# Three edits to a kernel of attention and two expert layers: weight loads behind the last maxima, the last tile's y in two parts, and one second layer ahead of transposes

## The chip, the cores and the metric

The kernel runs on one core of a Trainium2 chip. Its time is device microseconds (us) of one execution, median of several. The core has a matrix engine (TensorE, PE in the profile, its weight loads PEld), VectorE (DVE), ScalarE (ACT), GpSimd (POOL) and SyncE (SP), which here issues most of the transfers. Each engine works through a program of its own in order, and waits for the others by semaphores.

## The reference

Three stages follow each other, all in float32:

```python
def _attn_ref(q, k, v, f):            # (4, 8, 576, 64), f: (4, 8, 576)
    scores = q @ k.transpose(0, 1, 3, 2) / sqrt(D)
    cum = np.cumsum(np.log(np.clip(f, 0.0001, 1.0)), axis=-1)
    scores = np.where(causal, -1e9, scores + cum[..., :, None] - cum[..., None, :])
    scores = scores - np.max(scores, axis=-1, keepdims=True)
    attn = np.exp(scores)
    return attn / (np.sum(attn, axis=-1, keepdims=True) + 1e-09) @ v

def _moe_ref(x, w1, w2, w3, w_out):   # x: (2304, 512), w3: (1024, 1024)
    return ((x @ w1) * (x @ w2) @ w3) @ w_out

def _moe2_ref(x, w_gate, w_output_gate, w1, w2):   # 8 experts, 512 -> 1024 -> 512
    e_idx = np.argmax(x @ w_gate, axis=1)          # one expert for each row
    ...
    out[mask] = gate_w * eom * (np.maximum(x[mask] @ w1[e], 0.0) @ w2[e])
```

## The kernel before

**Precision.** Most operands are split in a high part (a reduced float32 form, fp32r) and a low part (the rest), and a product takes three matmuls: high by high, high by low, low by high (`three`, lines 549 to 551).

**Attention** goes over 16 pairs of heads, n = 0 to 15. What is done for a pair is cut into steps ("X0": scores of a row block, "m0": its maxima, "GA": the scores again, transposed, into PSUM group gA, "HA": the maxima and the decay added to it by matmuls from MR and CK, "eA": exponential, "a0": causal mask, "s1": block sums on POOL, "p0": product with v, "su": sums of the weights). Steps of one pair lie up to 90 us apart; each has a start time in `START`, pair n is 9.8 us behind pair n−1, and every engine's program is this list sorted by time. The last block of 64 queries is handled for both heads at once ("XL", tile xl). Its maxima end the row maxima of the pair: they are turned by a matmul and copied to the tile mt ("tc", ACT, line 253), and SP moves them into MR ("mv", line 183). gA's matmuls with MR and CK wait for that.

**The weights w3 and w_out** are multiplied with each other while attention runs, so that the gated layer needs one product y instead of two. They come in pieces of 512 KB (o0, 00, o1, ...; class `Combined`). A piece goes through seven steps, K0 to K6 (`narrow`, lines 449 to 467): SP loads it, ACT, DVE (lines 458, 460, 462) and ACT convert it from 64-bit to 32-bit floats, POOL takes the low part. `upto(step, n)` issues a step for the first n pieces. The raw buffers are three, so a load waits until DVE has read the piece three before it. In attention's program the steps of the pieces stand in the same list; those at its end stand in `AFTER`, in us after the start of the last pair: "K0_15" is the load of the 15th piece (w14), "K0_16" that of wo5, "K0_17" that of w05, "K4_13" and "K4_14" are the conversions of wo4 and w04. P0 to P3 are the first products of the two matrices.

**The gated layer** (`gated`) takes 512 rows at a time, the last tile (t=4) 256. For each f of eight it makes a and b, their product ga, and its parts gh and gl (`post`, on ACT and DVE). `project` then makes y for each chunk of 128 rows from all eight f (24 matmuls of 512 columns), copies it to a row tile xr with ACT, turns it by four transposes (`turn`), and, in `rest`, makes the logits; `route` finds the expert of each row and its place, and POOL scatters the rows into xs, sorted by expert. PSUM tiles of these stages come from five buffers in turn (`mmt`).

**The experts.** The most frequent expert m comes first: its first 256 rows ("A", `layer1`, then `layer2` with both chunks), then 128 more ("B", `features` with four transposes, `layer1_few`, `turn_few`, `layer2`), then the other seven. The order of PE's and DVE's work is as written here, with generators that are advanced by `take` and `run`; ACT, POOL and SP are ordered by a planner. `weights` asks for weight chunks of 512 KB, through three raw buffers; each `load` splits one on POOL and DVE. `fetch` brings rows from xs; those of B (xgB) are fetched on POOL's queue behind the scatter of the last tile's rows.

Of the kernel before, what the change touches and what calls it, by code (L numbers as in the profile page):

```python
# [11 lines left out]
F32 = mybir.dt.float32  # L12
# [15 lines left out]
E = 8  # L28
P = 128
# [32 lines left out]
FILL = {(0, "X0"): 5, (0, "XL"): 10, (1, "X0"): 4, (1, "XL"): 4, (2, "X2"): 5, (2, "X0"): 5}  # L62

AFTER = {
    "K4_13": 4.4, "K0_15": 4.41, "K0_16": 4.42, "K4_14": 4.43, "K0_17": 4.44, "inputs": 11.36, "scores": 13.38,
    "K1_15": 18.5, "K1_16": 18.51, "K4_15": 18.52, "K0_18": 18.53, "K4_16": 18.54, "P0": 28.29, "P1": 28.3, "P2": 28.31,
    "P3": 28.32,
}
# [449 lines left out]
def moe(nc, tc, ident, xT, rz, xs, xpool, raws, region, wc, w1, w2, gates, e1, e2, out):  # L518
# [3 lines left out]
    with (  # L522
# [12 lines left out]
        def mmt(name):  # L535
            return st["mm"].tile([P, 512], F32, name=name, tag="mm")

        def tmp(name):
            return st["work"].tile([P, 512], F32, name=name, tag="tmp", bufs=TMP if "moa" in st else 3)
# [5 lines left out]
        def three(ps, terms, start=True, stop=True):  # L545

            last = len(terms) - 1
            for i, ((ah, al), (bh, bl)) in enumerate(terms):
                PE.matmul(ps, ah, bh, start=start and i == 0, stop=False)  # L549
                PE.matmul(ps, ah, bl, start=False, stop=False)  # L550
                PE.matmul(ps, al, bh, start=False, stop=stop and i == last)  # L551

        TT = [512] * 4 + [N - 2048]
# [52 lines left out]
            return st["xr"][:, c % 2]  # L606

        def project(t, nc_):
            rows, lg = [], psr.tile([P, 4, 2 * E], F32, name=f"lg{t}", tag="r")
            if t == len(TT) - 1:  # L610
                x2t = [p2.tile([P, 2, P * nc_], F32, name=f"x2t{k}", tag="ga") for k in (0, 2)]
            else:
                x2t = [xT[:, k:k + 2, 512 * t:512 * t + P * nc_] for k in (0, 2)]

            def rows_of(c):
                cs = slice(P * c, P * c + P)
                ps = mmt(f"y{t}{c}")
                three(ps, [((gh[:, f, cs], gl[:, f, cs]), (wch[:, f], wcl[:, f])) for f in range(8)])
                rows.append(row_tile(t, c))
                A.activation(out=rows[c][:, :DM], in_=ps, func=ACTF.Copy)  # L620

            def turn(c):
                pt = psx.tile([P, 512], F32, name=f"xt{t}{c}", tag="x")
                for k in range(4):
                    PE.transpose(pt[:, P * k:P * k + P], rows[c][:, P * k:P * k + P], ident)
                for i, y in enumerate(x2t):
                    A.activation(out=y[:, :, P * c:P * c + P], in_=pt[:, 256 * i:256 * i + 256].rearrange("p (k c) -> p k c", k=2), func=ACTF.Copy)

            for c in range(nc_):
                rows_of(c)  # L630
                if c > 0:
                    turn(c - 1)

            def rest():
                turn(nc_ - 1)
                yield

                pt = psx.tile([P, 512], F32, name=f"lt{t}", tag="x")
                for k in range(4):
                    PE.matmul(pt[32 * k:32 * k + 32, :P * nc_], wg[:, k], x2t[k // 2][:, k % 2], start=True, stop=True)  # L640
                part = tmp(f"lp{t}")
                A.activation(out=part[:, :P * nc_], in_=pt[:, :P * nc_], func=ACTF.Copy)
                yield
                for c in range(nc_):
                    PE.matmul(lg[:, c], part[:, P * c:P * c + P], four, start=True, stop=True)
                yield
                yield from route(t, nc_, rows, lg)

            return rest()
# [78 lines left out]
        w1h, w1l, w2h, w2l, gh, gl = (unit(x, 8) for x in ("w1h", "w1l", "w2h", "w2l", "gh", "gl"))  # L728
# [6 lines left out]
        for hf, j in wc.steps:  # L735
# [12 lines left out]
            if j == 7:  # L748
                if hf == 0:
                    wch, wcl = (x.bitcast(F32R) for x in wc.raw)  # L750
# [7 lines left out]
        psr = psum.enter_context(tc.tile_pool(name="psr", bufs=1, space=PSUM, reuse_waits="tile"))  # L758
# [316 lines left out]
        def rows_of_expert(e, first=0):  # L1075
            return lambda r, n: by_expert[bass.ds(e, 1), first + r:first + r + n].rearrange("o n d -> (o n) d")

        def run(*steps):

            for x in steps:  # L1080
                for _ in x:
                    pass

        def take(x, n=1):
            for _ in range(n):
                next(x, None)

        m = nc.values_load(mi[0:1, 0:1], engines=[*SPE, POOL_E], min_val=0, max_val=E - 1)
        with tc.manual_schedule(engines={PE_E, DVE_E}):
            wm, gA = weights("m", m), fetch("A", rows_of_expert(m), 256)  # L1090
            fA = features("A", gA, 256)
            xA, hA = next(fA), hidden("A")
            rest = project(len(TT) - 1, TT[-1] // P)
            load(4)
            take(fA, 2)
            take(rest)
            take(fA, 2)
            take(rest)
            l1 = layer1("A", wm, xA, 256, hA)
            take(l1)  # L1100
            take(rest, 2)
            cn = count("")
            next(cn)
            take(l1, 2)
            run(rest)
            gB = fetch("B", rows_of_expert(m, 256), P, "xgB", 1, G)
            take(l1)
            load(1)
            take(l1)
            pl = plan(*next(cn))  # L1110
            load(1)
            take(pl)
            take(l1)
            load(1)
            take(l1)
            load(1)
            slots = [None] + [nc.values_load(tab[0:1, i:i + 1], engines=SPE, min_val=0, max_val=E - 1) for i in range(1, 3)]
            take(l1)
            ws = weights("1", slots[1])
            g = fetch("1", rows_of_expert(slots[1]), WIN[1])  # L1120
            run(l1)
            y = layer2("A", wm, gA, hA, 256)
            fB = features("B", gB, P)
            xB, hB = next(fB), hidden("B")
            take(y, 2)
            run(fB)
            run(y)
            load(2)
            hr = layer1_few("B", wm, xB)
            fx = features("1", g, WIN[1])  # L1130
            x = next(fx)
            take(fx, 2)
            turn_few("B", hr, hB)
            take(fx, 2)
            load(2)
            run(layer2("B", wm, gB, hB, P))
            load(1)
            h = hidden("1")
            l1 = layer1("1", ws, x, WIN[1], h)
            for _ in range(3):  # L1140
                take(l1, 1)
                load(1)
            slots += [nc.values_load(tab[0:1, i:i + 1], engines=SPE, min_val=0, max_val=E - 1) for i in range(3, E)]
            for i in range(1, E):
                nm, w = str(i), WIN[i]
                if i == E - 1:
                    pe0 = nc.values_load(tab[0:1, E:E + 1], engines=SPE, min_val=0, max_val=E - 1)
                    px0 = nc.values_load(tab[0:1, E + MAXP:E + MAXP + 1], engines=SPE, min_val=0, max_val=E * N - R)
                    nm2, e2_, w2_, rows2 = "p", pe0, R, lambda r, n: xs[bass.ds(px0, n)]
                else:  # L1150
                    nm2, e2_, w2_, rows2 = str(i + 1), slots[i + 1], WIN[i + 1], rows_of_expert(slots[i + 1])
                g2 = fetch(nm2, rows2, w2_)
                ws2 = (weights if i < E - 1 else plain)(nm2, e2_)
                if i > 1:
                    h = hidden(nm)
                    l1 = layer1(nm, ws, x, w, h)
                    take(l1)
                for k in range(4):
                    take(l1, 2 if i > 1 else 1)
                    load(1 if i < E - 1 else 0)  # L1160
                run(l1)
                fx = features(nm2, g2, w2_) if i < E - 1 else iter(())
                x = next(fx, None)
                take(fx, 2)
                y = (layer2_turned if w % P and w <= TURNED else layer2)(nm, ws, g, h, w)
                if i < E - 1:
                    take(y)
                    take(fx, 2)
                    for k in range(4):
                        load(1)  # L1170
                        take(y)
                        take(pl)
                else:
                    x = turned_piece("p", g2)
                    take(y)
                    p = piece("p", ws2, g2, x)
                    for _ in range(2):
                        take(p)
                        take(y)
                run(y)  # L1180
                ws, g = ws2, g2
            run(p)
# [61 lines left out]
```

## Time and profile before

| | |
|---|---|
| Time, median of 3 runs | 846.82 us (845.28 to 849.52) |
| The profiled execution | 848.34 us, its span 846.7 us |
| PE busy | 799.8 us, 94% |
| DVE, POOL, ACT busy | 451.4 us (53%), 376.2 us (44%), 281.3 us (33%) |
| Mean granted clock of PE | 0.986 of full speed |

Attention lasts until about 205 us, the products of the two weight matrices until about 262, the gated layer with y until about 580, the experts until the end. Times in the rows count from the start of the span. "L579" is line 579 of the kernel before.

### The profile page before, as it was taken

The numbers are of one execution on the slowest core, as the hardware profiler recorded it, in microseconds if no ns is written. First come the engines' busy times: TensorE is split into PE (matmuls) and PEld (weight loads), VectorE is DVE, ScalarE is ACT, GpSimd is POOL, SyncE is SP. The second block draws the span as 40 slices with busy tenths as digits, with TensorE's granted clock in tenths as the row PEclk, the third lists the DMA queues.
The fourth block names the chain that finished last, engine by engine and source line by source line (L and its number), as shares of the span: only waits on it lengthen the run. The fifth ranks groups of instructions, "written<-read, shape, count | busy, mean of one in ns | idle before, by whom it ended". The sixth has DMA issues, their size and how long they took to land.

```text
span 846.7 us, 13835 instructions
## 1 busy us (share of the span) xinstructions
PE 799.8 (94%) x5173; PEld 648.9 (77%) x5173; DVE 451.4 (53%) x950; ACT 281.3 (33%) x536; POOL 376.2 (44%) x383
## 2 busy tenths in 40 slices
PE   8999979969999899999999999999799999999995
PEld 4666656647886587787788788888588899999983
DVE  7788878862897841340423222245356846446530
ACT  2666656624354422212221221222122222322321
POOL 5688888875465550230113011032345443444521
PEclk9999999988999999999999999999999999999999
DMA  3455666521544220110100010043556654556460
GB/s 114 153 169 188 215 209 217 155 94 44 180 166 137 90 64 12 51 28 11 38 25 19 7 51 0 1 133 117 187 175 194 213 199 144 188 187 210 151 258 29
DMA packets 40340, 102.12 MB, mean 121 GB/s; under 512 B 8610, under 2 KB 9314, under 8 KB 40016
## 3 DMA queue, kind: packets, MB, share of 16 engines
q1 hardware_dynamic: 37088, 91.46, 33.9%
q0 software_dynamic: 3184, 9.77, 3.0%
q8 instruction: 41, 0.67, 0.3%
q14 instruction: 27, 0.22, 0.1%
HBM read 84.47 MB, written 16.51 MB: 119 GB/s over the span
## 4 chain that ended last, share of the span: by engine, by line
PE 60%; DVE 16%; DMA 11%; issue 7%; ACT 3%; SPq 2%; POOL 1%; POOLq 0%; DVEq 0%; ACTq 0%
DVE junk L243 5%; PE y L551 4%; PE y L550 4%; PE y L549 4%; PE h L551 3%; PE h L549 3%; PE h L550 3%; PE a L549 3%; PE b L549 3%; DMA xs<-xr,pos 3%; PE a L551 3%; PE a L550 3%; PE b L550 3%; PE b L551 3%; DMA out<-ot,id 3%
## 5 line engine op out<-in xcount | busy, mean ns | idle before, releaser
L579 DVE TENSOR_TENSOR ga<-b,ga 128x512 f32<-128x512 f32 (+1 forms) x40 | 25.4, 635 | 150.8 <-PE b L551 147.7
L694 POOL DMA_INDIRECT xs<-xr,pos x18 | 19.6, 1089 | 186.3 <-DVE pos L690 130.5
L243 DVE CUSTOM_DVE_ANT_0 junk<-x,tri 128x256 f32<-128x256 f32 (+3 forms) x128 | 62.7, 490 | 9.9 <-PE x L217 0.7
L549 PE MATMUL h<-gh,ah 128*128 128x320 f32 (+4 forms) x224 | 67.2, 300 | 0.0
L550 PE MATMUL h<-gl,ah 128*128 128x320 f32 (+4 forms) x224 | 66.9, 299 | 0.0
L551 PE MATMUL h<-gh,al 128*128 128x320 f32 (+4 forms) x224 | 66.9, 299 | 0.0
L551 PE MATMUL a<-xh,w1l 128*128 128x512 f32 (+1 forms) x160 | 59.9, 374 | 3.0 <-POOL w1l L467 3.0
L285 POOL TENSOR_SCALAR_AFFINE_SELECT PT<-PT 128x256 f32<-128x256 f32 (+1 forms) x80 | 44.9, 574 | 39.8 <-ACT PT L279 39.6
L549 PE MATMUL a<-xh,w1h 128*128 128x512 f32 (+1 forms) x160 | 60.7, 379 | 1.9 <-ACT w1h L465 1.9
L549 PE MATMUL b<-xh,w2h 128*128 128x512 f32 (+1 forms) x160 | 60.5, 378 | 0.0
L550 PE MATMUL b<-xl,w2h 128*128 128x512 f32 (+1 forms) x160 | 59.9, 375 | 0.0
L550 PE MATMUL a<-xl,w1h 128*128 128x512 f32 (+1 forms) x160 | 59.9, 374 | 0.0
L549 PE MATMUL y<-raw,gh 128*128 128x512 f32 x144 | 58.2, 404 | 1.3 <-ACT gh L580 1.3
L551 PE MATMUL b<-xh,w2l 128*128 128x512 f32 (+1 forms) x160 | 59.4, 371 | 0.0
L542 POOL TENSOR_SCALAR bh<-rb 128x1024 fp32r<-128x1024 f32 x28 | 37.6, 1342 | 48.1 <-DMA rb<-e 43.0
L551 PE MATMUL y<-raw,gl 128*128 128x512 f32 x144 | 57.4, 399 | 0.9 <-DVE gl L582 0.9
L550 PE MATMUL y<-raw,gh 128*128 128x512 f32 x144 | 57.8, 401 | 0.0
L580 ACT ACTIVATE gh<-ga 128x512 fp32r<-128x512 f32 (+1 forms) x40 | 23.6, 590 | 95.4 <-DVE ga L579 95.4
L306 PE MATMUL v<-PT,vr 128*64 128x448 f32 (+4 forms) x384 | 50.6, 401 | 1.1 <-ACT zs L329 1.1
L970 DVE SCALAR_TENSOR_TENSOR hl<-h,hh 128x320 fp32r<-128x320 f32 (+4 forms) x56 | 25.5, 463 | 48.6 <-ACT hh L969 47.7
L297 POOL TENSOR_TENSOR ac<-ac,PT 128x640 f32<-128x640 f32 (+1 forms) x32 | 45.2, 1414 | 1.6
L543 DVE TENSOR_TENSOR bl<-rb,bh 128x1024 fp32r<-128x1024 f32 x28 | 37.7, 1370 | 15.0 <-POOL bh L542 15.0
(612 smaller groups left out, 2204.3 us busy)
## 6 DMA issues: line engine op xcount, KB each, us to landing
ra<-e SPq DMA_DIRECT2D x28, 512.0 KB
rb<-e SPq DMA_DIRECT2D x28, 512.0 KB
w<-w3t SPq DMA_DIRECT2D x16, 512.0 KB
xs<-zero SPq DMA_DIRECT2D x8, 771.0 KB
vr<-v SPq DMA_DIRECT2D x16, 320.0 KB
kr<-k SPq DMA_DIRECT2D x16, 288.0 KB
qr<-q SPq DMA_DIRECT2D x16, 288.0 KB
wo<-wo SPq DMA_DIRECT2D x8, 512.0 KB
```

Source lines behind the costliest of these rows:

```text
L243: V.tensor_tensor_reduce(out=junk[:, :w], in0=s["x", i][:, 512 * h:512 * h + w] if i < 4 else s["x", i][:, 224:224 + S], in1=tri[:, 640 - ...
L285: G.affine_select(out=t, in_=t, pattern=[[0, 2], [1, w]], compare_op=ALU.is_ge, fill=0.0, base=0, channel_multiplier=-1,)
L297: G.tensor_tensor(out=acc[:, :, q0 - P:], in0=first if j == 1 else acc[:, :, q0 - P:], in1=src, op=ALU.add)
L306: PE.matmul(s["v"][HALF[h], 384 + q0:384 + q1], s["vr"][:, j, HALF[h]], place(s, j, h, q0, q1), start=(j == 0), stop=(j == 4 or q1 == P),)
L542: G.tensor_scalar(out=hi, in0=src, scalar1=1.0, scalar2=1.0, op0=ALU.mult, op1=ALU.mult)
L543: lo_eng.tensor_tensor(out=lo, in0=src, in1=hi.bitcast(F32), op=ALU.subtract)
L549: PE.matmul(ps, ah, bh, start=start and i == 0, stop=False)
L550: PE.matmul(ps, ah, bl, start=False, stop=False)
L551: PE.matmul(ps, al, bh, start=False, stop=stop and i == last)
L579: V.tensor_tensor(out=ga[:, :w], in0=pb[:, :w], in1=ga[:, :w], op=ALU.mult)
L580: A.activation(out=gh[:, f, :w], in_=ga[:, :w], func=ACTF.Copy)
L970: V.scalar_tensor_tensor(out=hl[:, f, :w], in0=ps[:, :w], scalar=0.0, in1=hh[:, f, :w].bitcast(F32), op0=ALU.max, op1=ALU.subtract)
```

## The change

Three edits. In `AFTER` the loads of the pieces w14, wo5 and w05 go from 4.41, 4.42 and 4.44 to 6.70 to 6.72, behind the last pair's "mv" (6.59); the conversion K4_14 stays. In `project` the last tile's two chunks are both summed over f = 0 to 6 first, each in its own PSUM tile, and then each over f = 7; the matmuls are the same. In the expert stage the second layer of the 256 rows (A) is issued whole before the four transposes of the 128 rows (B); before, three quarters of it went ahead of them and one quarter, 12 matmuls, behind.

```diff
 AFTER = {
-    "K4_13": 4.4, "K0_15": 4.41, "K0_16": 4.42, "K4_14": 4.43, "K0_17": 4.44, "inputs": 11.36, "scores": 13.38,
+    "K4_13": 4.4, "K4_14": 4.43, "K0_15": 6.7, "K0_16": 6.71, "K0_17": 6.72, "inputs": 11.36, "scores": 13.38,
...
         def project(t, nc_):
-            rows, lg = [], psr.tile([P, 4, 2 * E], F32, name=f"lg{t}", tag="r")
+            part, rows, lg = [], [], psr.tile([P, 4, 2 * E], F32, name=f"lg{t}", tag="r")
...
+            def sums_of(c, ps, fs):
+                cs = slice(P * c, P * c + P)
+                three(ps, [((gh[:, f, cs], gl[:, f, cs]), (wch[:, f], wcl[:, f])) for f in fs], fs[0] == 0, fs[-1] == 7)
+
             def rows_of(c):
-                cs = slice(P * c, P * c + P)
-                ps = mmt(f"y{t}{c}")
-                three(ps, [((gh[:, f, cs], gl[:, f, cs]), (wch[:, f], wcl[:, f])) for f in range(8)])
+                if t < len(TT) - 1:
+                    ps = mmt(f"y{t}{c}")
+                    sums_of(c, ps, range(8))
+                else:
+                    if c == 0:
+                        part.extend(mmt(f"y{t}{i}") for i in range(nc_))
+                        for i in range(nc_):
+                            sums_of(i, part[i], range(7))
+                    ps = part[c]
+                    sums_of(c, ps, range(7, 8))
                 rows.append(row_tile(t, c))
...
             xB, hB = next(fB), hidden("B")
-            take(y, 2)
+            run(y)
             run(fB)
-            run(y)
             load(2)
```

## Rows read from the trace of the kernel before

**Rows 1.** The page's engine table: busy us (share of the span) xinstructions

```profile
PE 799.8 (94%) x5173; PEld 648.9 (77%) x5173; DVE 451.4 (53%) x950; ACT 281.3 (33%) x536; POOL 376.2 (44%) x383
```

**Rows 2.** Waits of weight loads from 612 us: total us, times, longest

```profile
PEld gt L954 <- issue: 2.7, 16, 0.2
```

**Rows 3.** Windows: us; PE, PEld, DVE, ACT, POOL busy; PEclk; DMA share; GB/s

```profile
190.80:196.00 5.20, 5.14 (x38) 4.76 (x38) 0.00 (x0) 2.65 (x3) 1.06 (x3) 0.50 0.14 53
196.00:201.00 5.00, 4.42 (x42) 2.42 (x40) 0.00 (x0) 1.24 (x2) 4.75 (x5) 0.84 0.00 0
...
600.00:602.00 2.00, 0.56 (x2) 0.24 (x2) 1.33 (x2) 0.00 (x0) 0.64 (x1) 1.00 1.00 404
...
573.00:576.00 3.00, 3.00 (x8) 2.32 (x8) 1.17 (x2) 0.60 (x1) 1.81 (x3) 0.52 0.98 325
...
610.50:613.50 3.00, 3.00 (x10) 2.32 (x9) 2.04 (x5) 0.71 (x4) 2.78 (x3) 0.52 0.12 44
```

**Rows 4.** Timeline of SP at attention's end: start us, duration, instruction

```profile
174.60 0.39 SPq L449 DMA_DIRECT2D w<-w3t  x1
...
186.60 0.33 SPq L449 DMA_DIRECT2D w<-w3t  x1
...
187.50 1.16 SPq L183 DMA_DIRECT2D MR<-mt  x2
```

**Rows 5.** Timeline of all engines, n=14 and n=15: [idle before <-releaser]

```profile
178.87 0.27 ACT L253 ACTIVATE mt<-xl 9x128 fp32r<-9x128 f32 x1 [1.18 <-issue]
...
181.86 0.29 PE L217 MATMUL gA<-ql,kh 64*128 64x288 f32 x2
...
190.86 0.82 PE L217 MATMUL gA<-MR,CK 64*128 64x192 f32 x4 [8.71 <-DMA MR<-mt]
...
195.98 3.71 PE L306 MATMUL v<-PT,vr 128*64 128x128 f32 x24
...
201.51 2.92 PE L306 MATMUL v<-PT,vr 128*64 128x128 f32 x24 [1.10 <-ACT zs L329]
...
205.09 0.50 PE L513 MATMUL wc<-cw 128*128 128x512 f32 x1
```

**Rows 6.** Timeline of PE, the same matmuls for n=14

```profile
173.94 0.41 PE L217 MATMUL gA<-MR,CK 64*128 64x192 f32 x4
...
176.65 0.40 PE L235 MATMUL xl<-kh,QD 128*128 128x288 f32 x1
```

**Rows 7.** Chain of waits behind attention, one weight load: start us, us, what

```profile
213.90 4.67 DMA w<-w3t
```

**Rows 8.** Timeline of DVE, the first conversion behind the three loads

```profile
202.08 0.43 DVE L458 TENSOR_SCALAR w14u<-w14u 128x512 int32<-128x512 int32 x1 [15.00 <-ACT w14u L456]
```

**Rows 9.** Timeline of PE and ACT at the last tile's y

```profile
564.55 0.39 PE L549 MATMUL y<-raw,gh 128*128 128x512 f32 x1
...
569.21 0.40 PE L551 MATMUL y<-raw,gl 128*128 128x512 f32 x1
...
570.89 0.50 PE L549 MATMUL y<-raw,gh 128*128 128x512 f32 x1 [1.28 <-ACT gh L580]
...
572.50 0.50 PE L551 MATMUL y<-raw,gl 128*128 128x512 f32 x1 [0.87 <-DVE gl L582]
...
579.99 0.60 PE L625 MATMUL xt<-ident,xr 128*128 128x128 f32 x4
580.19 0.60 ACT L620 ACTIVATE xr<-y 128x512 f32<-128x512 f32 x1 [6.50 <-PE y L551]
```

**Rows 10.** Timeline around the transposes of the 128 rows

```profile
610.00 0.66 PE L954 MATMUL gtB<-ident,xgB 128*128 128x128 f32 x4 [3.84 <-DMA xgB<-xs]
...
610.42 0.79 ACT L955 ACTIVATE ghB<-gtB 128x128 fp32r<-128x128 f32 x4 [5.91 <-PE gtB L954]
...
610.73 0.89 DVE L956 TENSOR_TENSOR glB<-gtB,ghB 128x128 fp32r<-128x128 f32 x4 [8.50 <-ACT ghB L955]
...
614.84 0.39 PE L549 MATMUL hB<-ahm,ghB 128*128 128x512 f32 x1
```

## The prediction

> **What bounds the kernel now.** I read the page's engine table first: TensorE (PE) is busy for 94% of the span [rows 1], so a change pays only where it removes time in which PE stands still or runs slowly. Next the waits of PE and of its weight loads by stretch. Between 545 and 612 us PE waits at the two places that the second and third edit touch (below); from 612 us to the end its weight loads stand longest in all before the transposes, 16 times and at most 0.2 us each [rows 2], so what is gained before 612 us should arrive at the end. The windows view then gives the clock: in three stretches PE is at the half level (1.2 GHz, shown as 0.50), each time behind a stretch in which it stood [rows 3]. The three edits lie at these three places. The timelines of SyncE (SP), PE, ScalarE (ACT) and GpSimd (POOL) give the working below.
>
> **Edit 1, three loads go behind the last row of maxima.** SP issues in program order and waits inside the queue. The maxima of the last pair (n=15) are ready in mt at 178.87 + 0.27 = 179.14, but their copy to MR is issued at 187.50 [rows 4, 5]: ahead of it stand three 512 KB weight loads, of which the third leaves only at 186.60, since its raw buffer is first read out by VectorE (DVE). PE has finished the other terms of gA at 181.86 + 0.29 = 182.15 and stands until 190.86 [rows 5].
> After the edit the queue before the maxima holds only the load of v for n=14 (due 5.71; the maxima are due 6.59, the loads 6.70). SP issues the MR copies at about 179.17. From first issue to matmul it took 190.86 − 187.50 = 3.36 us; from 179.17 that is 182.53. PE waits 0.4 instead of 8.7 us: **8.3 us**, or all 8.7 if the copy, with no large transfer ahead of it, lands sooner.
> The clock adds to that. From the MR part of gA to the first matmul behind gD the slow pass takes 195.98 − 190.86 = 5.1 us; the same matmuls of n=14 took 176.65 − 173.94 = 2.7 us [rows 5, 6]: 2.4 us lost. From 196 to 201 the mean clock is 0.84 [rows 3], that is 5 × 0.16 / 0.5 = 1.6 us at half level, 0.8 us lost. With 0.4 us of standing instead of 8.7 I take the clock to stay up: **3.2 us**, bounds 0 and 3.2.
> What comes late next: v of n=15. Its load stands behind the third weight load, which does not move (it waits for DVE's conversion, not for SP's order), so it leaves at about 187.6 (186.60 + 0.33, then a store and the load itself, an issue taking about half of the 1.16 us of the MR pair [rows 4]). The product that needs it starts at 201.51 now; after the edit at 182.5 + 2.7 + 3.6 (a product and its sums, 205.09 − 201.51) + 1.1 in which ACT empties the PSUM buffer [rows 5], or 189.9. A load took up to 4.67 us from issue to landing [rows 7], so it lands by 192.3 at the latest; 320 KB is less than the 512 KB of that row, but one such load is in front of it. I take 190.4: **0.5 us** given back, bounds 0 and 2.4. POOL's block sums of n=15 start when PE's scores come, so they move along.
> The cost of the delayed loads: the first leaves at about 180.4 instead of 174.60, and lands by 185.1 by the 4.67 us. Its conversion on DVE stood for 15.0 us until 202.08 [rows 8], not for the load but for ACT, whose copy of it comes in program order behind its work on the n=14 product; that moves ahead to about 191. Slack 5 us, so it costs nothing; without that cover it would cost what it is late. The other two loads leave when DVE frees their buffers, as before.
> Behind 205.09, where the combining products begin, PE, DVE's conversion and the loads are one chain started by the end of attention; all of it moves. Sum of edit 1: 8.3 + 3.2 − 0.5 = **11.0 us**; bounds 8.3 − 2.4 = 5.9 and 8.7 + 3.2 = 11.9.
>
> **Edit 2, the last tile's y in two parts.** y's matmuls follow at (569.21 − 564.55)/20 = 0.233 us [rows 9]. The f=7 terms of chunk 0 wait twice, 1.3 and 0.9 us [rows 9], for gh and gl; gl comes late because DVE has a weight split in front of it. Then the clock is down, 0.52 from 573 to 576 [rows 3], and the first transpose starts at 579.99. After: both chunks' f=0 to 6, 42 matmuls, fill 564.55 to 574.33, past gl, which the f=7 matmul got at 572.50; six more end the issue at 575.73. No wait, and no fall of the clock.
> The edit adds one wait: chunk 0's sum ends only three matmuls before the transposes. Its last matmul starts at 564.55 + 44 × 0.233 = 574.80 and ends some 0.4 later; ACT's copy takes 0.60 [rows 9], so the transpose starts at about 575.9. Gain 579.99 − 575.9 = **4.1 us**; bounds 2.2 (the two waits alone) and 4.3 (the copy hidden). Both PSUM tiles come from five buffers whose earlier contents were read out long before; queued behind the waiting transpose are only transposes of the expert rows, which have landed. The routing of the last tile, its scatter and the fetch of 128 rows that edit 3 speaks of start from here, and move by the same 4.1.
>
> **Edit 3, the second layer ahead of the transposes.** Now PE waits at the transposes of xgB for 3.84 us until 610.00, with 12 ready matmuls of oA behind them; these then run at half clock, and hB starts at 614.84 [rows 3, 10]. After: the 12 run in the wait (12 × 0.233 = 2.8 us), 1.1 us of it stays, the transposes start at 610.00 again (counted against the same landing) and take 0.66. The cover that the 12 gave to ACT and DVE is gone: hB needs the first copy, ghB, at 610.42 + 0.2, and the low parts at a pace of 0.89/4 = 0.22 us from 610.73, while hB asks for a new one each 0.7 us. hB starts at about 610.7: **4.1 us**; bounds 1.8 (hB waits for all four low parts, 611.6, and the clock falls, below) and 4.2. No DMA is moved but the scatter of oA's second chunk, which is ready earlier; one GpSimd scatter of about 1 us ahead of a weight copy has the slack of the next layer's loads.
> The remaining 1.1 us is where the Trainium skill speaks against me: "TensorE: Matmul & The Clock Gate", section "HAM oscillation — how this bites in real kernels", says that a wait for a transfer between bursts of matmuls drops the clock, so that each burst starts cold. The trace agrees for the 3.84 us wait; by this rule the sum would be 17.8, by the row 600 to 602, 19.2.
> The row that decides for me is the stretch 600 to 602: PE busy 0.56 of 2 us, around two waits, and the clock stays at 1.00 [rows 3]. I take no fall.
>
> **Sum.** 11.0 + 4.1 + 4.1 = 19.2 us. The profiled execution took 848.34 us (span 846.7), giving 829.1; it stands 1.5 above the median 846.82, from which the sum gives 827.6. I forecast 828. The bounds together give 9.9 and 20.4, from the median 837 and 826.
>
> **Rivals.**
> *The clock falls behind the 1.1 us that stays.* The 12 matmuls at the fallen clock took 614.84 − 610.66 = 4.2 instead of 2.8: 1.4 us lost, 829.4; if it also falls behind the 1.6 us around v of n=15, as much again, 831. For it: falls came behind waits of 2.2 and 3.8 us. Against: 600 to 602.
> *Edit 1 gains nothing at the end.* Conversion, not PE, sets the pace from 205 to 300 us, and loads that come no sooner keep it where it was; or another entry still holds the maxima up. Then 8.2 us stay: 839. Half of it: 834. For: the chain there runs through DVE and loads. Against: DVE had stood 15.0 us for ACT [rows 8], and each load waits for DVE, so they move together.
> *Slower.* The delayed loads starve the conversion at attention's end. It decides only if the first load, now issued at 180.4, lands so late that DVE starts on it after 202.08 and the 8.2 us of the other edits, so if it takes over 29 us; at 33 us the kernel is 4 us slower, about 851. The row seen has 4.67.
>
> **How the numbers follow.** The forecast 0.72 (826 to 831), the fallen clock 0.12 (829 to 832), edit 1 lost or half lost 0.12 (833 to 840), slower 0.04. The range takes the first two and the better part of the third: 825 to 836. A measurement of this kernel tells about 0.5% (4.2 us) from no change; the first three cases are all faster by more than that, less something for a sum that is wrong altogether: faster 0.92, same 0.04, slower 0.04.
>
> **What would show it.** In the changed kernel: MR's issue near 179.2 and the wait of gA under 1 us; no half clock between 182 and 198; the combining products from about 194.1 rather than 205.09; y without a wait for gh or gl and a short one before its first transpose; one wait of about 1 us for xgB, no half clock behind it, hB some 19 us earlier than 614.84; from there all the same. Wrong if PE's waits between 262 and 300 grow by what edit 1 gave, if v of n=15 lands well after 191, or if waits appear after 612 because weights no longer come in time.

## The result and the profile after

The changed kernel takes 833.26 us, median of 4 runs (832.18 to 833.81), beside 847.18 us (845.28 to 849.52) for the kernel before, also of 4 runs. The ratio is 0.983 (0.981 to 0.985): it is 13.9 us faster. The profiled execution took 832.97 us with a span of 831.3, so the two profiled executions differ by 15.4 us. The 1.5 us between the two figures is where the profiled ones happen to lie: that of before 1.2 above its median here, that of after 0.3 below.

The table cuts the profiled executions where the three edits act. All entries are us; "falls" names the waits from 180 us on behind which the granted clock was at half level: v (the product of n=15), y, o (second layer of the 256 rows), x (behind the wait for xgB). The last microseconds, behind the last matmul, are at half level in every profile and are left out. A star marks another run of the same program; the kernels below the third row of the changed one are those of the experiments. Each row is one execution, and "none" holds for that one.

| | first combining product | to y | y to its transposes | to hB | to the end | falls |
|---|---|---|---|---|---|---|
| before | 205.09 | 359.46 | 15.44 | 34.85 | 231.84 | MR's wait, y, x |
| before* | 204.50 | 360.50 | 13.45 | 34.16 | 231.89 | MR's wait, x |
| changed | 197.03 | 359.40 | 11.40 | 31.63 | 231.87 | v, o |
| changed* (second) | 196.14 | 359.44 | 11.41 | 31.46 | 231.89 | v, o |
| changed* (third) | 197.88 | 359.51 | 11.40 | 30.16 | 231.89 | v |
| loads only | 197.96 | 359.39 | 15.41 | 34.49 | 231.79 | v, y, x |
| y only | 204.87 | 360.64 | 11.40 | 35.42 | 231.84 | MR's wait, x |
| second layer only | 204.65 | 359.43 | 13.60 | 31.02 | 231.95 | MR's wait |
| one load behind | 200.42 | 359.45 | 15.83 | 35.15 | 231.84 | MR's wait, y, x |
| v ahead | 194.19 | 360.69 | 11.41 | 30.38 | 231.99 | none |
| v ahead* | 194.24 | 360.39 | 11.42 | 30.07 | 231.97 | none |
| v ahead, zeros | 195.67 | 359.54 | 11.41 | 30.38 | 231.97 | none |
| PE kept busy | 195.68 | 359.54 | 11.41 | 30.33 | 231.87 | none |
| split on ACT | 195.17 | 360.76 | 11.42 | 31.35 | 233.14 | x |

Changed against before: 8.06 + 0.06 + 4.04 + 3.22 − 0.03 = 15.35 us. From hB on the two kernels are alike, so everything gained ahead of it arrives at the end.

The page's engine table of the changed kernel shows the same instructions in less time, PE 2.4 us less busy and the rest of the 15.4 us less idle [rows 1]:

```profile
PE 797.4 (96%) x5173; PEld 646.6 (78%) x5173; DVE 456.7 (55%) x950; ACT 280.6 (34%) x536; POOL 375.9 (45%) x383
```

First edit. SP's timeline of the changed kernel at attention's end: start, duration, instruction. The MR copies are issued 8.3 us sooner than in [rows 4], the weight loads follow as buffers come free, and v's load of n=15 leaves behind the last of the three.

```profile
179.21 1.14 SPq L183 DMA_DIRECT2D MR<-mt  x2
180.44 0.34 SPq L449 DMA_DIRECT2D w<-w3t  x1
...
186.94 0.33 SPq L449 DMA_DIRECT2D w<-w3t  x1
...
187.98 0.34 SPq L188 DMA_DIRECT2D vr<-v  x1
```

The timeline of PE, ACT and POOL over the same stretch, with the idle time before an instruction and its releaser in brackets:

```profile
182.04 0.41 PE L217 MATMUL gA<-MR,CK 64*128 64x192 f32 x4
184.75 2.92 PE L306 MATMUL v<-PT,vr 128*64 128x128 f32 x24
...
188.99 0.40 ACT L329 ACTIVATE zs<-v 128x288 f32<-128x288 f32 x1
190.94 3.25 POOL L297 TENSOR_TENSOR ac<-ac,PT 128x640 f32<-128x640 f32 x2
191.93 4.44 PE L306 MATMUL v<-PT,vr 128*64 128x128 f32 x24 [3.54 <-DMA vr<-v]
...
197.03 0.50 PE L513 MATMUL wc<-cw 128*128 128x512 f32 x1
```

The 8.71 us in front of gA [rows 5] are gone without a rest, and the product of n=14, 195.98 before, starts at 184.75, 11.2 us sooner. Of these, 3.2 are lost again at the product of n=15: it stands 3.54 us for v's load, and then its first 24 matmuls take 4.44 us against 2.92 in [rows 5].

Windows of the changed kernel: us; PE, PEld, DVE, ACT, POOL busy; PEclk; DMA share; GB/s. The first three lines are the end of attention, the last two the second layer of the 256 rows.

```profile
182.00:186.00 4.00, 4.00 (x50) 3.22 (x48) 3.93 (x4) 3.41 (x5) 3.84 (x4) 1.00 0.65 237
188.00:192.00 4.00, 0.46 (x16) 0.21 (x6) 1.89 (x3) 2.05 (x4) 3.83 (x4) 0.95 0.60 206
192.00:195.00 3.00, 3.00 (x12) 1.46 (x14) 2.97 (x3) 0.00 (x0) 2.12 (x2) 0.50 0.20 46
...
590.00:592.00 2.00, 2.00 (x7) 1.63 (x8) 0.19 (x1) 0.03 (x1) 0.05 (x1) 0.75 0.63 103
592.00:594.00 2.00, 2.00 (x6) 1.52 (x6) 0.00 (x0) 0.66 (x1) 0.59 (x1) 0.50 0.66 239
```

The clock stays up at gA, and falls to half behind v's wait and again at 591.

Second edit. PE, PEld, ACT and DVE at the last tile's y:

```profile
556.43 0.39 PE L549 MATMUL y<-raw,gh 128*128 128x512 f32 x1
...
563.50 0.41 DVE L582 TENSOR_TENSOR gl<-ga,gh 128x256 fp32r<-128x256 f32 x1
...
567.18 1.24 ACT L631 ACTIVATE xr<-y 128x512 f32<-128x512 f32 x2 [4.88 <-PE y L551]
567.39 0.40 PE L551 MATMUL y<-raw,gl 128*128 128x512 f32 x1
567.83 0.43 PEld L636 LDWEIGHTS xt<-ident,xr 128*128 128x128 f32 x4 [0.48 <-ACT xr L631]
567.83 0.66 PE L636 MATMUL xt<-ident,xr 128*128 128x128 f32 x4
```

Both waits of [rows 9] are gone: gl is ready at 563.91, and the f=7 terms that read it come behind 42 matmuls, at about 566.2. The one new wait, for ACT's copy, is 0.48 us.

Third edit. The timeline from the 256 rows' second layer to hB:

```profile
588.65 0.50 PE L549 MATMUL oA<-bhm,hhA 128*128 128x512 f32 x1 [1.14 <-POOL bhm L542]
589.91 0.50 PE L550 MATMUL oA<-blm,hhA 128*128 128x512 f32 x1 [0.76 <-DVE blm L543]
...
597.49 0.18 POOL L950 CAST idB<-xgB 128x1 int32<-128x1 f32 x1 [4.90 <-DMA xgB<-xs]
...
598.30 0.60 PE L965 MATMUL gtB<-ident,xgB 128*128 128x128 f32 x4
598.55 0.69 ACT L1046 ACTIVATE otA<-oA,gtA 128x512 f32<-128x512 f32 x1 [5.89 <-PE oA L551]
599.13 0.78 ACT L966 ACTIVATE ghB<-gtB 128x128 fp32r<-128x128 f32 x4
599.46 0.50 PE L549 MATMUL hB<-ahm,ghB 128*128 128x512 f32 x1 [0.56 <-ACT ghB L966]
```

xgB has landed at 597.49, but PE reaches the transposes only at 598.30: the matmuls before them ran slowly, behind the two short waits at 588 to 590. The 3.84 us of [rows 10] are gone, and 0.56 us before hB are new, because ACT takes the copy otA before ghB.

### The profile page after: what moved, and what is told of

It reads as the page before. It is cut to its first block, busy times and chain, and to the rows that moved or that the text cites. A ratio compares the mean times of both kernels' runs of the same rounds, so it can differ in the third digit from the quotient of the medians.

```text
span 831.3 us, 13837 instructions
## 1 busy us (share of the span) xinstructions
PE 797.4 (96%) x5173; PEld 646.6 (78%) x5173; DVE 456.7 (55%) x950; ACT 280.6 (34%) x536; POOL 375.9 (45%) x383
## 4 chain that ended last, share of the span: by engine, by line
PE 72%; DVE 13%; issue 7%; DMA 4%; ACT 2%; SPq 1%; POOL 1%; DVEq 0%; POOLq 0%; ACTq 0%
DVE junk L243 6%; PE y L550 4%; PE y L549 4%; PE y L551 4%; PE h L551 3%; PE h L549 3%; PE h L550 3%; PE b L549 3%; PE a L549 3%; PE b L550 3%; PE a L551 3%; PE a L550 3%; PE b L551 3%; PE q L549 2%; PE q L551 2%
## 5 line engine op out<-in xcount | busy, mean ns | idle before, releaser
L542 POOL TENSOR_SCALAR bh<-rb 128x1024 fp32r<-128x1024 f32 x28 | 34.9, 1246 | 48.1 <-DMA rb<-e 37.7
L306 PE MATMUL v<-PT,vr 128*64 128x448 f32 (+4 forms) x384 | 52.3, 411 | 3.5 <-DMA vr<-v 3.5
```

Of the source, the lines that this page charges most:

```text
L306: PE.matmul(s["v"][HALF[h], 384 + q0:384 + q1], s["vr"][:, j, HALF[h]], place(s, j, h, q0, q1), start=(j == 0), stop=(j == 4 or q1 == P),)
L542: G.tensor_scalar(out=hi, in0=src, scalar1=1.0, scalar2=1.0, op0=ALU.mult, op1=ALU.mult)
```

## The experiments

**Each edit alone.** Three kernels, each the kernel before with one edit.

> The first edit alone. Theory: the edits add, and this one carries 8.1 us to the end, the amount by which the combining products start sooner in the changed kernel (197.03 against 205.09 us); v's product of the last pair waits 3.5 us for its load and the clock falls behind that. About 839 us. Rival, conversion sets the pace from 205 to 300 us: less than 8 arrives, 842 to 847, and PE's waits between 262 and 300 grow.

> The second edit alone. Theory: the first transpose behind y comes 4.1 us sooner (1.3 and 0.9 us of waits and the fallen clock behind them) and all of it arrives: about 843 us; hB then starts 4.1 us sooner than 614.84. Rival, the later scatter and fetch of the 128 rows do not move along (they wait for earlier transfers): hB only gains what PE gains, nothing at the end, 847.

> The third edit alone. Theory: hB starts 0.7 to 0.8 us behind the first transpose as soon as xgB has landed, whatever the clock does before; where the clock does not fall in the second layer, as in the kernel before, 4.1 us sooner (610.7), about 843 us; where it falls there as in the changed kernel, 3.2 us, about 844. Rival, the price of the missing cover is what took 0.9 us of this edit: 3.2 us at full clock too.

Measured, against 847.23 for the kernel before: loads 840.23 (ratio 0.991, 0.988 to 0.994), y 845.06 (0.996, 0.995 to 0.998), second layer 844.16 (0.997, 0.995 to 0.998). That is 7.0, 2.2 and 3.1 us, 12.2 together beside 13.9 for the whole change; the interval of the loads alone reaches 2.5 us to either side, so the edits add within the noise. With the loads alone the product of n=15 stands for v and runs slowly, as in the changed kernel; PE's timeline of that run:

```profile
191.54 5.60 PE L306 MATMUL v<-PT,vr 128*64 128x128 f32 x24 [3.41 <-DMA vr<-v]
...
197.96 0.50 PE L513 MATMUL wc<-cw 128*128 128x512 f32 x1
```

So this loss belongs to the first edit. The y edit alone has its full effect, 11.40 us to the transposes (table), but the median gains 2.2 us where I expected 4.1. The second layer's profile shows one reason: it has the old y, with both its waits (1.00 and 0.88 us), and yet took 13.60 us, not 15.44. Its window behind these waits is at full clock:

```profile
574.00:578.00 4.00, 4.00 (x20) 3.22 (x19) 1.23 (x1) 0.12 (x1) 2.36 (x3) 1.00 0.69 226
```

The third edit alone does behind the landing of xgB what I expected. The transposes and hB in that run:

```profile
607.94 0.66 PE L954 MATMUL gtB<-ident,xgB 128*128 128x128 f32 x4 [1.31 <-DMA xgB<-xs]
...
608.70 0.50 PE L549 MATMUL hB<-ahm,ghB 128*128 128x512 f32 x1
```

From the landing, which starts the transposes here and before, to hB it takes 0.76 us instead of 614.84 − 610.00 = 4.84 [rows 10]: 4.1 us less. So the missing cover costs nothing; the rival is out.

**The loss at v.** Two theories of the missing 3 us: the place of v's load in SP's queue, behind the third weight load, and the clock that falls behind the wait. The first kernel is the changed one with v's load of the last pair ahead of the three weight loads; the second keeps the load where it is and has 14 matmuls of zeros, which add nothing to the output, in the wait.

```diff
-SHIFT = {}
+SHIFT = {(15, "lv"): 6.65 - 15.51}
```
```diff
                 fn, *args = stages[x]
+                if (n, x) == (15, "p0"):
+                    for _ in range(14):
+                        PE.matmul(wc.acc[0][0], z[:, :P], z, start=True, stop=True)
```

> The changed kernel with the load of v for the last pair issued directly behind the maxima, ahead of the three weight loads. Theory A, this load and the clock are all that the first edit lacks: no wait for v, no half clock, combining products at 193.1 instead of 197.03, 4 us less than the changed kernel, about 829 us. Theory B, behind v stand POOL's block sums, done at 194.2 in the changed kernel: the sums wait for them, products at about 194.9, 2.1 us less, about 831. Rival, v's load is late because of the traffic and not because of its place in the queue: it lands no sooner, nothing changes.

> The changed kernel with 14 matmuls of zeros (3 us, into a PSUM tile that is cleared later) ahead of the last pair's product with v. Theory: the wait for v's load stays (the product starts at about 191.9), but the clock does not fall behind it, and product and sums take 3.6 us instead of 5.1: combining products at 195.5 instead of 197.03, 1.5 us less than the changed kernel, about 831.7. Rival, the clock falls whatever PE does in front, or the sums wait for POOL until 194.2 anyway with nothing gained: 833.

Measured: v ahead 830.22 us (0.979, 0.977 to 0.982), PE kept busy 830.05 (0.979, 0.976 to 0.982). Timeline of the kernel with v ahead, SP, PE and POOL:

```profile
180.61 0.33 SPq L188 DMA_DIRECT2D vr<-v  x1
...
189.50 2.92 PE L306 MATMUL v<-PT,vr 128*64 128x128 f32 x24 [1.10 <-ACT zs L329]
190.42 2.99 POOL L297 TENSOR_TENSOR ac<-ac,PT 128x640 f32<-128x640 f32 x2
...
194.19 0.50 PE L513 MATMUL wc<-cw 128*128 128x512 f32 x1
```

Timeline of the kernel with PE kept busy:

```profile
188.25 0.34 SPq L188 DMA_DIRECT2D vr<-v  x1
...
192.11 2.92 PE L306 MATMUL v<-PT,vr 128*64 128x128 f32 x24 [0.20 <-DMA vr<-v]
...
195.68 0.50 PE L516 MATMUL wc<-cw 128*128 128x512 f32 x1
```

With v there in time the product starts at 189.50, so in the changed kernel v costs 191.93 − 189.50 = 2.4 us of wait. With PE kept busy that wait is there (192.11) but not the fall: 24 matmuls take 2.92 us, and the combining products come 197.03 − 195.68 = 1.35 us sooner. Its windows over the wait and the product, at full clock:

```profile
188.00:192.00 4.00, 3.91 (x33) 1.78 (x30) 1.48 (x3) 2.07 (x4) 3.83 (x5) 1.00 0.63 214
192.00:195.00 3.00, 2.89 (x28) 1.85 (x30) 2.97 (x3) 0.00 (x0) 2.40 (x2) 1.00 0.12 18
```

So the place in the queue and the clock each cause a part of the loss. The rival, traffic, is out: v was there in time once it was issued ahead. Of what the two profiles gain over that of the changed kernel, 1.3 us is something else: both lack the fall in the second layer (30.4 and 30.3 us to hB instead of 31.6), where neither edit acts.

The waits of PE and PEld in the kernel with v ahead show what comes next: us in total, times, longest.

```profile
PE v L322 <- POOL ac L297: 1.1, 1, 1.1
...
PEld b L549 <- DVE raw L765: 0.8, 1, 0.8
...
PE gtB L965 <- DMA xgB<-xs: 0.4, 1, 0.4
```

Of the 3.9 us (2.4 + 1.5) only 2.84 arrive at the combining products, since the sums of the weights now wait 1.1 us for POOL's block sums, which end at 193.41. And from there to y it takes 360.69 instead of 359.40 us: a wait of 0.8 us for DVE (line 765, the low part of the combined weights), which the changed kernel doesn't have, and 0.6 us more of waits for w1h from ACT. It would be natural to read this as conversions that now set the pace, but the second profile of the kernel before, in which attention ends 10 us later, has the same wait and takes 360.50 us:

```profile
PEld b L549 <- DVE raw L754: 0.6, 1, 0.6
```

The y edit alone takes 360.64 us, and the kernel of the next experiment, with v ahead too, 359.54. What decides between about 359.5 and 360.6 the runs don't show.

**Is it the clock at POOL's wait?** The kernel with v ahead, with four matmuls of zeros each at the product and at the sums, against the same kernel without them and the changed kernel, on one chip:

```diff
+                if (n, x) in ((15, "p0"), (15, "su")):
+                    for _ in range(4):
+                        PE.matmul(wc.acc[0][0], z[:, :P], z, start=True, stop=True)
```

> v's load ahead, and four matmuls of zeros each in PE's two short waits at attention's end (about 0.9 us each). Theory: these waits cost only their length, so where the clock does not fall without the filling, nothing changes: as the kernel with v ahead, 829 to 830.5. Rival, the clock falls there in most executions: 1 to 1.5 us less.

> The kernel with v's load ahead once more, beside the changed kernel. Theory: 2 to 3 us less than it, 829 to 830.5, the combining products near 194.2, held by POOL's block sums for about 1 us. Rival, the first look was a lucky one: no difference from the changed kernel.

> The changed kernel, unaltered, beside the two versions with v's load ahead, on one chip. 832 to 833.5 us, half clock again behind the wait for v.

Measured: with the zeros 831.42 us (0.981, 0.979 to 0.983), v ahead 829.70 (0.980, 0.978 to 0.982), changed 833.35 (0.984, 0.982 to 0.987). The zeros bring nothing, and neither profile of the kernel with v ahead has a fall there without them. That holds for the profiled executions: two of the five of this kernel took 831.49 and 832.54 us, at a mean granted clock of 0.992 and 0.990 against 0.994 to 0.996 in the other three, so the clock fell somewhere in them. The changed kernel with v ahead lies 3.0 to 3.7 us below the changed one, with intervals that touch or overlap slightly; it can't be told from the one in which PE is kept busy (830.05).

**The place in the queue.** The kernel before with only one of the three loads behind the maxima:

```diff
-    "K4_13": 4.4, "K0_15": 4.41, "K0_16": 4.42, "K4_14": 4.43, "K0_17": 4.44,
+    "K4_13": 4.4, "K0_15": 4.41, "K0_16": 4.42, "K4_14": 4.43, "K0_17": 6.72,
```

> The kernel before with only the third of the three loads behind the maxima. Theory, the copy to MR costs what it stands behind in SP's queue: MR is issued when the second load has left, at 183.2, gA's matmuls start 3.3 us later at 186.5, so PE waits 4.3 us instead of 8.7; the clock falls there, for a shorter time than before; v's load of the last pair lands as in the changed kernel at about 192 and is waited for by at most 1 us. Combining products at 197 to 200, so 5 to 8 us less than before, 839 to 842. Rival, the transfers of the loads and not the queue held MR up: MR lands no sooner than before, nothing gained.

Measured: 842.33 us (0.994, 0.991 to 0.996), 5.3 us below the 847.63 of before on that chip. Its timeline, SP and PE:

```profile
182.93 1.16 SPq L183 DMA_DIRECT2D MR<-mt  x2
...
186.32 0.83 PE L217 MATMUL gA<-MR,CK 64*128 64x192 f32 x4 [5.04 <-DMA MR<-mt]
```

The maxima now leave behind the second load's buffer, and part of the wait stays: 5.0 us, where I expected 4.3, and the combining products at 200.42 lie just outside my 197 to 200. From MR's issue to gA it takes 3.4 us in both kernels (186.32 − 182.93, and 190.86 − 187.50 before), so it is indeed the load at the queue's head and not the traffic that held them up.

**The same programs again**, for how far the falls of the clock differ between executions:

> The kernel before once more, unaltered. Theory as for the changed kernel: the same waits (8.7 us for the maxima, 1.3 and 0.9 at y, 3.8 for the 128 rows), the clock behind y low in some executions and not in others, so that from y's first matmul to the first transpose it takes 15.4 or 13.6 us. Rival, low again behind each of the three, 15.4. Median about 847.

> The changed kernel once more, unaltered. Theory, whether the clock falls behind a pair of waits of about 1 us (in the second layer of the 256 rows) or behind the wait for v is settled anew in each execution: the waits come out the same to 0.3 us, but falls of 3.4 us stand at other places, and hB starts 30.4 us behind the first transpose of y where there is none, 31.6 where there is one. Median 832 to 834. Rival, falls belong to the program: again at about 191.6 and 591.

Measured: before 846.92 us (ratio 1.000, 0.999 to 1.002), changed 832.09 (0.983, 0.980 to 0.986). The kernel before, profiled again, has no fall behind y's waits, but neither are the waits the same, as I had expected: the first is 0.85 us instead of 1.28. First PE's waits of that run, then the window behind them:

```profile
PE y L551 <- DVE gl L582: 0.9, 1, 0.9
PE y L549 <- ACT gh L580: 0.8, 1, 0.8
```
```profile
574.00:578.00 4.00, 4.00 (x19) 3.20 (x18) 1.23 (x1) 0.00 (x0) 2.09 (x2) 1.00 0.75 252
```

The changed kernel fell in its second layer in this run, as in the first, and did not in the third (the one of 833.35 above). The same window of the second and of the third run:

```profile
590.00:594.00 4.00, 4.00 (x12) 3.12 (x11) 0.00 (x0) 0.69 (x1) 0.64 (x1) 0.58 0.76 210
```
```profile
590.00:594.00 4.00, 3.25 (x14) 2.66 (x15) 1.03 (x2) 0.69 (x1) 0.64 (x1) 1.00 0.77 225
```

The waits ahead of it are alike: 0.94 and 0.77 us in the second run, 1.02 and 0.75 in the third. My expectation that the falls would lie elsewhere in the second run was wrong. Over all profiles, 13 have these two waits (0.7 to 1.2 us and 0.8), and the clock fell behind them in two, both of the changed kernel; the length doesn't tell them apart, since it stayed up behind 1.2 us.

At y it is otherwise. Of the five profiles with the old y, the clock fell in the three whose first wait was 1.25, 1.28 and 1.67 us (15.4 to 15.8 us to the transposes), and stayed up in the two with 0.85 and 1.00 (13.5 and 13.6); the second wait is 0.9 in all five. Whether the longer wait brings the fall no experiment here tried.

**Taking the two short waits away.** The kernel with v ahead, in which ACT and not POOL makes the high part of the weight chunk that oA waits for:

```diff
-            load(1)
+            load(1, True)
             slots = [None]
...
+                if act:
+                    A.activation(out=hi, in_=raw, func=ACTF.Copy)
+                    V.tensor_tensor(out=lo, in0=raw, in1=hi.bitcast(F32), op=ALU.subtract)
```

> The kernel with v's load ahead, and with the high part of the last weight chunk for the 256 rows made on ACT, so that it does not stand behind the last tile's scatter on POOL. Theory, the third edit is bounded by the landing of the 128 rows: the two waits in the second layer (0.9 and 0.8 us) shrink, the wait for the 128 rows grows by as much, hB starts 30.4 us behind y's first transpose as in the kernel with v ahead; nothing gained but what a clock fall there costs, 829 to 830. Rival, those waits set hB's start: 1 us or more sooner, 29 us behind, 828.

Measured: 833.58 us (0.985, 0.982 to 0.987), slower than v ahead (0.979 and 0.980). Of the 3.2 us between the profiled executions 1.0 were there before the edit's place, at the first combining product; 2.1 lie from xt on. The two waits are gone, and PE waits for xgB instead. The transposes in the kernel with v ahead, and then in this one with the windows around them:

```profile
595.91 0.66 PE L965 MATMUL gtB<-ident,xgB 128*128 128x128 f32 x4 [0.44 <-DMA xgB<-xs]
```
```profile
597.95 0.96 PE L970 MATMUL gtB<-ident,xgB 128*128 128x128 f32 x4 [3.94 <-DMA xgB<-xs]
```
```profile
594.00:598.00 4.00, 0.06 (x2) 0.05 (x1) 0.00 (x0) 0.69 (x1) 0.04 (x1) 1.00 0.71 254
598.00:601.00 3.00, 3.00 (x9) 2.33 (x10) 2.04 (x5) 0.85 (x4) 2.78 (x5) 0.53 0.00 0
```

The landing of xgB ends this stretch, and hB follows it by 0.75 us in both kernels. The two waits in front of it cost nothing by themselves. Of the 2.1 us, 1.0 is a later landing, 30.6 us behind the first transpose of y instead of 29.6 (between 29.3 and 30.4 in the other profiles); why, and whether the edit does it, the runs don't show. The other 1.1 stand behind hB, where the matmuls run at half clock behind the one long wait.

## Why the prediction was right and where it was wrong

The direction and the three mechanisms were right, and 833.3 lies in the forecast's range (825 to 836), but not where I put the likeliest case (826 to 831). Between the profiled executions the sum was 19.2 and the gain 15.4; the other 1.5 + 0.3 us of the distance from 827.6 to 833.26 are where the profiled executions lie about their medians. That the range holds the result is in part luck: its upper end was there for the rival in which half of the first edit is lost to the conversion (834), and what the runs show at that time is a wait for v and two falls of the clock.

**Edit 1, the wait of gA: right.** MR issued at 179.21 (forecast 179.17), gA at 182.04 (182.53) without a wait, clock up.

**Edit 1, what comes late next: the step that failed.** "I take 190.4: 0.5 us given back." The load left at 187.98 (187.6) and let the product start at 191.93, 3.9 us later, where my value left it 2.8; the row of 4.67 us was the nearer bound. The wait cost 2.4 us, the bound I had named. Behind it the clock fell, 1.5 us more: 5.10 us from the product to the combining products against 3.57 with PE kept busy. The edit gave 8.06 instead of 11.0. The rival of the fallen clock named this place at 1.4 us; it was right there in every profile with v's wait of 3.3 to 3.5 us. The prediction counted 1.6 us of standing there (1.1 and 0.5) and gave the falls a chance of 0.12; with 3.3 to 3.5 us one came four times of four.

The Trainium skill, "TensorE: Matmul & The Clock Gate", section "HAM oscillation — how this bites in real kernels", tells of bursts that start cold behind a wait for a transfer, in its case of about 3 to 5 us. The traces agree for a wait of that length, 0.50 behind 3.54 us, and 1.00 where the wait was filled. What I took from it for 1.1 us that section doesn't say, and behind the 1.31 us for xgB in the second layer only the clock stayed at 1.00.

**Edit 1, POOL: off, hidden in this kernel.** "They move along" holds only until 193.41, where the block sums end: with v in time the sums wait 1.1 us for them. That the combining products then start at 194.19, where I had put them (194.1), is luck: another limit gives the same time.

**Edit 1, nothing lost behind 205: right.** To y it takes 359.40 against 359.46. The 1.0 to 1.3 us more of the kernel with v ahead are no sign of the rival "conversion sets the pace", since the kernel before has them too in one of its two profiles.

**Edit 2: right.** 4.04 us (4.1), new wait 0.48. But the 15.44 of before holds a fall of the clock that not every execution has; where it is missing the edit is worth 13.5 − 11.4 = 2.1 us, about the lower bound, and about what it gave alone in the median. The no-fall part of the forecast was right for the new y in all its profiles.

**Edit 3: mechanism right, 3.22 us against 4.1.** "The row that decides for me is the stretch 600 to 602 ... I take no fall." The clock fell all the same, behind the two short waits of that stretch and before the one I thought of. The matmuls ended 0.8 us behind the landing, and hB waited for ghB behind another copy of ACT. Where it did not fall, hB followed the landing by 0.74 to 0.76 us, against 4.84 before, which is the 4.1 of the forecast. Counted from xt it is, in the changed kernel and those with v ahead or PE kept busy, 4.5 to 4.8 us less than the 34.85 of before, because the landing came 0.4 to 0.7 us sooner behind xt than the 30.01 there. To take no fall was the likelier choice, with 11 of the 13 profiles for it, but one stretch of one execution couldn't show that.

**Open.** Why the clock falls behind the second layer's two waits in one execution and not in another the runs don't show, nor whether the fall at y hangs on its longer wait. Nor was it tried to make POOL's block sums faster, which come next at attention's end.

## What to carry to other kernels

When a transfer is moved out of the way of a waiting one in an in-order queue, follow what stands behind it too: here the next load, unmoved, became the new wait, and moving it as well brought the combining products 2.8 us sooner. Price a load that is due at once by the longest row of a load seen, and count a fall of the clock behind it if PE waits as long as waits that had one: here each of the 15 waits of 3.3 us or more did. A gain read from one profile holds that execution's falls of the clock: compare the segments of two profiles of the same program before a per cent is shared out among edits, and before a loss behind an edit is put down to it.

## What the runs showed of the hardware that was not expected

The same program has different falls of TensorE's clock from execution to execution, behind waits that are alike to 0.1 us: the changed kernel fell behind 0.94 and 0.77 us in its second layer and not behind 1.02 and 0.75, 31.5 or 30.2 us to hB. Two waits of about 1 us each, between stretches of dense matmuls, can therefore be followed by a fall to 1.2 GHz, and mostly were not, in 11 of 13 profiles. At y, where the first of two waits differed, the falls went with the longer one (1.25 to 1.67 us against 0.85 and 1.00).

All 15 waits of PE of 3.3 us or more between 180 us and the last matmul of a profile (for MR, v and xgB) were followed by a fall. Filling one of them with matmuls of zeros kept the clock at 1.00.
